# One tile instead of two for expert 0's later tokens, and the last routing rounds ahead of expert 0's first tile

## The chip, the cores and the metric

One core of one Trainium2 chip. The metric is the device time of one execution in microseconds (us), as the median of several runs. Engines are named as in the profile: PE (TensorE, the matmuls), PEld (its weight loads), DVE (VectorE), ACT (ScalarE), POOL (GpSimd), SP (SyncE, here a queue that issues transfers).

## What is computed

The reference is a decayed linear attention over 4 sequences of 768 tokens with 8 heads of 64 features, whose output is the input of a mixture of 16 experts in 4 groups:

```python
state = gamma[None, :, None, None] * state + np.einsum('bhd,bhe->bhde', k[:, :, t], v[:, :, t])
y[:, :, t] = scale * np.einsum('bhd,bhde->bhe', q[:, :, t], state)
...
g_idx = np.argmax(x @ w_group, axis=1)
e_idx = np.argmax(xg @ w_expert[g], axis=1)
h = np.maximum(xg[mask_e] @ w1[g, e], 0.0)
ye = h @ w2[g, e]
out[tok_idx] = (g_w[mask_g][mask_e] * e_w[mask_e])[:, None] * ye
```

All is float32 outside; there are 3072 tokens of 512 features, and an expert's two weight matrices (512 x 1024 and 1024 x 512) are 4 MB.

## The kernel before

**Attention and routing.** The attention takes 12 steps, each of two chunks of 128 tokens (`attention`, L851; 24 chunks in all). One step later the chunk's output is transposed back and stored to a DRAM tensor `xd` (`trans_mm`, `x_store` L289), and its router logits are formed: `logits_mm`, a copy by ACT, then `logits` (L312). Both logits steps write the same PSUM tile `log`. After every four chunks a routing round runs (`route` L325; six rounds): some six DVE operations that find group and expert, then five small matmuls that rank the tokens within each expert (`rk`), then some thirteen DVE operations that give each token its slot. `route_steps` issues the first part up to the word "wait" and, at its next call, the second. The slots go to POOL, which scatters each chunk's token numbers and gains into the lists `meta` (`enlist` L422).

**Expert 0 and expert 1 start early.** Their tokens of the first 12 chunks (`EARLY`) form tiles `ua` and `va` of 128 columns, which are worked on while the attention ends. Expert 0's later tokens form `ub` (88 columns, chunks 12 to 19, `MIDDLE` = 20) and `uc` (50 columns, chunks 20 to 23), expert 1's form `vb` (128 columns). A table gives chunk limit, width and list number:

```python
EARLY, MIDDLE = (12, 20)
PARTS = [
    [(EARLY, 128, 0), (MIDDLE, 88, NX), (NCH, 50, NX + 1)],
    [(EARLY, 128, 1), (NCH, 128, NX + 2)],
]
```

**A tile.** `listed` (L603) loads a tile's list on SP's queue, `gather` (L618) fetches the tokens by an indirect transfer that POOL issues, `xtrans` (L631) transposes them on PE into PSUM, from where ACT writes `xh` (float16) and DVE the rest `xl` (bfloat16). `layers` (L648) is a generator: four groups (`f2`) of 24 matmuls for the first layer, each of the three products wh.xh, wh.xl and wl.xh for four blocks of k and two halves `a`; after a group ACT writes `hh` and DVE `hl`. It stops after each half. Then the second layer, in one of two forms: with more than 116 columns (`TMAJ`) 24 matmuls of 512 columns (L714), else 96 matmuls that give the transposed result (L738), which `ytrans` (L764) turns back. `result` scales the rows and `scatter` writes them to the output through POOL. Transposes, first-layer groups and rank matmuls take turns in four PSUM slots (tag "big").

**Weights.** `wload` reads an expert's 4 MB in four transfers into four buffers on SP's queue, `wload_part` in sixteen. `wsplit` (L591) makes from a part `wh` (ACT) and then `wl` = wf - wh (DVE); a buffer is free for the next expert when its parts are split. Expert 0 is split in sixteen parts (k = 0 to 15, of which 9 to 15 fall in the stretch of the change), expert 1 in eight.

**The fourteen others.** When all tokens are counted, `order` (L436) ranks the experts by their number of tokens, ten DVE operations on one row that end with `ord`. `picked` (L577) lets SP read an entry of it; only then can the weights and the list of `us[0]` be asked for, and so on for 14 tiles of 256 down to 173 columns. A final loop (`general` L802) takes what did not fit in a tile.

**Order.** The program's order is kept on every engine (`manual_schedule`), so `run` (L937) fixes all queues. Behind the attention's last step it has: the logits matmuls of the last step, one group of `ua`, the transposes and stores, the list of `ub`, the first part of the sixth routing round, the last four splits of expert 0, the loads of expert 1's last two buffers, two groups of `ua`, the second part of the round and its four scatters, the gather of `ub`, the lists of `uc` and `vb`, the transposes of `va`, four splits of expert 1, the ranking and the first two loads of `us[0]`, the second layer of `ua`; then `va` (with four more splits), `ub`, `uc`, `vb` (with the splits of `us[0]` and, after its first-layer groups 1 and 2, the transposes of `us[0]`), and the loop over `us`. In the attention's last step, the first group of `ua` and three splits stand ahead of the transposes and the second part of the fifth round. One DRAM dependency is released by hand for `ub` (groups "middle" and "late"): its list and gather don't wait for what later chunks write.

Of the kernel before, what the change touches and what calls it, by code (L numbers as in the profile page):

```python
# [14 lines left out]
ALU = mybir.AluOpType  # L15
# [24 lines left out]
EARLY, MIDDLE = (12, 20)  # L40
PARTS = [
    [(EARLY, 128, 0), (MIDDLE, 88, NX), (NCH, 50, NX + 1)],
    [(EARLY, 128, 1), (NCH, 128, NX + 2)],
# [3 lines left out]
NP = NX + 3  # L47
PW = WIDTH + [PARTS[1][0][1], PARTS[0][0][1], PARTS[0][1][1], PARTS[0][2][1], PARTS[1][1][1]]
# [44 lines left out]
class Kernel:  # L93
# [195 lines left out]
    def x_store(self, i, s):  # L289

        nc, tc, st = self.nc, self.tc, self.st[i]
# [3 lines left out]
        d = nc.sync.dma_start(self.xd[t0:t0 + P, :], xr)  # L295
        if 2 * i >= MIDDLE:
            tc.add_to_no_dep_group("late", d.ins)
# [124 lines left out]
    def enlist(self, slot, src, c):  # L422
# [9 lines left out]
        if self.done > MIDDLE:  # L432
            tc.declare_no_dep(i.ins, group="middle", reason="no later token enters this list")
            tc.add_to_no_dep_group("middle", i.ins)
# [156 lines left out]
    def wsplit(self, u, k, n=8, eng=None):  # L591
# [3 lines left out]
        if h == 0:  # L595
# [7 lines left out]
    def listed(self, u, group=None, eng=None):  # L603

        nc, tc, bp = self.nc, self.tc, self.bp
# [4 lines left out]
        eng = eng or nc.sync  # L610
        for i, r in enumerate(rows):
            m = self.meta[u["seg"]] if static else self.meta[bass.ds(u["e"], 1)].rearrange("o r c -> (o r) c")
            d = eng.dma_start(mt[0:r, i, :], m[i * P:i * P + r, :])
            if group:
                tc.declare_no_dep(d.ins, group=group, reason="no later token enters this list")
                tc.add_to_no_dep_group(group, d.ins)

    def gather(self, u, group=None):  # L618
        nc, mt = self.nc, u["mt"]
        u["xg"] = xg = self.xg[u["at"][0]][:, u["at"][1]:, :]  # L620
        for i, r in enumerate(u["rows"]):
            n = u.get("tokens", NT)
            d = nc.gpsimd.indirect_dma_start(  # L623
# [4 lines left out]
            if group:  # L628
                self.tc.declare_no_dep(d.ins, group=group, reason="no token of these chunks is in the list")
# [18 lines left out]
    def layers(self, u):  # L648
# [6 lines left out]
        for f2 in range(4):  # L655
            ps = pp.tile([P, 512], F32, name="hps", tag="big", bufs=4)
            hv = ps.rearrange("p (a t) -> p a t", a=2)
            for a in range(2):
# [192 lines left out]
    def attention(self, extra, beside):  # L851
# [28 lines left out]
        for i in range(NST):  # L880
# [27 lines left out]
            if i >= 1:  # L908
# [28 lines left out]
    def run(self):  # L937
        tc, nc = self.tc, self.nc
        with ExitStack() as ctx:
# [14 lines left out]
            (ua, ub, uc), (va, vb) = [  # L954
                [dict(e=e, W=w, seg=l, tokens=c * P if c == EARLY else NT, pool=wpool[e]) for c, w, l in parts] for e, parts in enumerate(PARTS)
            ]
            for i, u in enumerate((ua, va, ub, uc, vb)):
                u["at"] = (0, i % 2)
            us = [dict(at=((j + 1) % 2, 0), W=WIDTH[j], pool=wpool[j % 2]) for j in range(NS)]
# [23 lines left out]
            def beside(i, place):  # L983
# [4 lines left out]
                if i == NST - 1:  # L988
# [173 lines left out]
```

## Time and profile before

| | us |
|---|---|
| median of 3 runs | 444.26 (443.36 to 444.46) |
| the profiled execution, device time | 442.78 |
| its span, first to last instruction | 441.0 |
| PE busy | 413.9 (94%) |
| DVE busy | 291.7 (66%) |
| ACT busy | 216.1 (49%) |
| POOL busy | 160.5 (36%) |

Times in the rows are microseconds from the span's start. Matmuls are pipelined: a row's second number is the time that the profile gives to an instruction or a merged group, and the distance of two starts is what an instruction costs in a dense run. "issue" is a wait for nothing that the profile shows. The granted clock is a share of 2.4 GHz; 0.50 is 1.2 GHz.

### The profile page before, as it was taken

The numbers are of one execution on the slowest core, as the hardware profiler recorded it, in microseconds if no ns is written. First come the engines' busy times: TensorE is split into PE (matmuls) and PEld (weight loads), VectorE is DVE, ScalarE is ACT, GpSimd is POOL, SyncE is SP. The second block draws the span as 40 slices with busy tenths as digits, with TensorE's granted clock in tenths as the row PEclk, the third lists the DMA queues.
The fourth block names the chain that finished last, engine by engine and source line by source line (L and its number), as shares of the span: only waits on it lengthen the run. The fifth ranks groups of instructions, "written<-read, shape, count | busy, mean of one in ns | idle before, by whom it ended". The sixth has DMA issues, their size and how long they took to land.

```text
span 441.0 us, 13102 instructions
## 1 busy us (share of the span) xinstructions
PE 413.9 (94%) x5502; PEld 337.1 (76%) x5502; DVE 291.7 (66%) x495; ACT 216.1 (49%) x345; POOL 160.5 (36%) x134
## 2 busy tenths in 40 slices
PE   7989999888798879999999999999999999999991
PEld 4878898677765867857788897978978879779770
DVE  3648568465696207968598976769668687696610
ACT  1132242234673327736474655757567567676520
POOL 4443855742354131422324350613504315222010
PEclk9999999999899969999999999999999999999996
DMA  8999999996657635977667777668887788876001
GB/s 271 417 325 410 351 394 365 302 270 196 242 192 246 225 89 201 297 265 240 233 238 268 252 275 300 222 257 261 309 311 261 257 286 293 295 289 253 27 9 34
DMA packets 37104, 112.76 MB, mean 256 GB/s; under 512 B 14095, under 2 KB 14735, under 8 KB 29363
## 3 DMA queue, kind: packets, MB, share of 16 engines
q1 hardware_dynamic: 25587, 98.08, 62.8%
q0 software_dynamic: 10496, 13.14, 9.4%
q8 instruction: 44, 0.72, 0.6%
q10 hardware_dynamic: 960, 0.68, 0.5%
q14 instruction: 17, 0.14, 0.1%
HBM read 99.47 MB, written 13.81 MB: 257 GB/s over the span
## 4 chain that ended last, share of the span: by engine, by line
PE 82%; issue 6%; DVE 4%; DMA 4%; ACT 1%; POOL 1%; POOLq 0%; DVEq 0%; ACTq 0%
PE hps L666 30%; PE yps L689 13%; PE yps L694 8%; PE yps L714 7%; PE sc L208 5%; PE op L269 5%; PE tpx L643 3%; PE tp L287 2%; PE stp L229 2%; DMA k<-kb 2%; PE op L257 2%; DVE wl L601 2%; PE yps L738 2%; PE log L305 1%; PE tpy L775 1%
## 5 line engine op out<-in xcount | busy, mean ns | idle before, releaser
L601 DVE TENSOR_TENSOR wl<-wf,wh 128x1024 bf16<-128x1024 f32 (+1 forms) x131 | 150.5, 1175 | 57.5 <-ACT wh L600 43.0
L666 PE MATMUL hps<-xbh,wl 128*128 128x128 f16 (+16 forms) x608 | 138.0, 244 | 1.3 <-issue 1.3
L666 PE MATMUL hps<-xbl,wh 128*128 128x128 bf16 (+16 forms) x608 | 138.0, 244 | 1.2 <-DVE xbl L646 1.2
L666 PE MATMUL hps<-xbh,wh 128*128 128x128 f16 (+16 forms) x608 | 138.1, 244 | 0.1
L600 ACT ACTIVATE wh<-wf 128x1024 f16<-128x1024 f32 (+1 forms) x136 | 130.7, 1000 | 0.4 <-DMA wf<-w2p 0.4
L666 PEld LDWEIGHTS <-wh 128*128 128x128 f16 x1216 | 105.5, 99 | 4.2 <-issue 1.0
L794 POOL DMA_INDIRECT out<-yo,mt x33 | 40.1, 1216 | 184.9 <-ACT yo L759 100.9
L623 POOL DMA_INDIRECT xg<-xd,mt x33 | 56.6, 1714 | 27.9 <-DMA mt<-meta 15.9
L671 ACT ACTIVATE hh<-hps 128x256 f16<-128x256 f32 (+16 forms) x76 | 35.7, 471 | 61.1 <-PE hps L666 58.0
L666 PEld LDWEIGHTS <-wl 128*128 128x128 bf16 x608 | 59.8, 99 | 3.7 <-issue 3.0
L672 DVE SCALAR_TENSOR_TENSOR hl<-hps,hh 128x256 bf16<-128x256 f32 (+16 forms) x76 | 40.1, 530 | 32.3 <-ACT hh L671 32.0
L694 PEld LDWEIGHTS <-wh 128*128 128x128 f16 x704 | 44.1, 98 | 20.8
L694 PE MATMUL yps<-hl,wh 128*128 128x103 bf16 (+10 forms) x352 | 44.3, 197 | 0.0
L694 PE MATMUL yps<-hh,wl 128*128 128x103 f16 (+10 forms) x352 | 44.3, 197 | 0.0
L694 PE MATMUL yps<-hh,wh 128*128 128x103 f16 (+10 forms) x352 | 44.2, 197 | 0.0
L215 DVE TENSOR_TENSOR pf<-sc,tri 128x512 f32<-128x512 f32 x48 | 30.0, 683 | 19.3 <-PE sc L208 16.8
L759 ACT ACTIVATE yo<-yps,mt 128x512 f32<-128x512 f32 x17 | 11.7, 687 | 57.1 <-PE yps L689 41.2
L426 POOL DMA_INDIRECT meta<-src,slot x24 | 24.7, 1031 | 37.4 <-DVE slot L418 32.1
L240 ACT ACTIVATE V<-stp 128x512 f32<-128x512 f32 x10 | 6.0, 597 | 65.6 <-PE stp L229 65.6
L689 PE MATMUL yps<-wh,hh 128*128 128x512 f16 x88 | 33.4, 379 | 0.0
L689 PE MATMUL yps<-wh,hl 128*128 128x512 f16 x88 | 33.3, 379 | 0.0
L689 PE MATMUL yps<-wl,hh 128*128 128x512 bf16 x88 | 33.3, 379 | 0.0
(139 smaller groups left out, 615.3 us busy)
## 6 DMA issues: line engine op xcount, KB each, us to landing
wf<-w1p SPq DMA_DIRECT2D x30, 1024.0 KB
wf<-w2p SPq DMA_DIRECT2D x30, 1024.0 KB
kk<-kkb SPq DMA_DIRECT2D x12, 512.0 KB
xd<-xr SPq DMA_DIRECT2D x24, 256.0 KB
k<-kb SPq DMA_DIRECT2D x11, 512.0 KB
q<-qb SPq DMA_DIRECT2D x11, 512.0 KB
v<-vb SPq DMA_DIRECT2D x11, 512.0 KB
wf<-w1p SPq DMA_DIRECT2D x8, 256.0 KB
```

Source lines behind the costliest of these rows:

```text
L215: nc.vector.tensor_tensor(st["pf"][:, s, par], st["sc", s, par].rearrange("p (g t) -> p g t", g=4), tri, ALU.mult)
L426: i = nc.gpsimd.indirect_dma_start(out=self.metaf, out_offset=bass.IndirectOffsetOnAxis(ap=slot[:, c:c + 1], axis=0), in_=src[:, c, :], in ...
L600: nc.scalar.activation(u["wh"][i][:, cs], u["wf"][i][:, cs], AF.Copy)
L601: (eng or nc.vector).tensor_tensor(u["wl"][i][:, cs], u["wf"][i][:, cs], u["wh"][i][:, cs], ALU.subtract)
L623: d = nc.gpsimd.indirect_dma_start(out=xg[0:r, i, :], out_offset=None, in_=self.xd[0:n, :], in_offset=bass.IndirectOffsetOnAxis(ap=mt[0:r, ...
L666: nc.tensor.matmul(hv[:, a, 0:W], l[:, k, fs], r[:, k, 0:W], start=(n == 0), stop=(n == 11))
L671: nc.scalar.activation(hh[:, f, 0:W], hv[:, :, 0:W], AF.Relu)
L672: nc.vector.scalar_tensor_tensor(hl[:, f, 0:W], hv[:, :, 0:W], 0.0, hh[:, f, 0:W], ALU.max, ALU.subtract)
L689: nc.tensor.matmul(ps, l[:, k, 0:P], m[k], start=(k == 0 and n == 0), stop=(k == 7 and n == 2))
L694: nc.tensor.matmul(yv[:, d, 0:r], l[g][:, ds], m[:, g, P:P + r], start=(g == 0 and n == 0), stop=(g == 7 and n == 2))
L714: nc.tensor.matmul(ps[0:r, :], l[:, k, ts], m[k], start=(n == 0), stop=(n == 23))
L794: s = nc.gpsimd.indirect_dma_start(out=self.out, out_offset=bass.IndirectOffsetOnAxis(ap=mt[0:r, i, 0:1].bitcast(U32), axis=0), in_=yo[0:r ...
```

## The change

Expert 0's tokens of the last twelve chunks become one tile of 128 columns, `ub`; `uc`, `MIDDLE` and the dependencies released by hand go. In the attention's last step the logits come ahead of the stores, and the first group of `ua` with its splits comes later, so that the second part of the fifth round stands ahead of it. Behind the attention, half a group of `ua` is followed by the last step's logits, transposes, logits of the routing and stores; the sixth round's first part comes ahead of three halves of `ua`'s groups, and its second part ahead of the last four splits of expert 0. A split can be issued in halves (`part`: "h" for ACT's, "l" for DVE's). For `ua` and `va` the twelve terms of a half group are sorted so that those with the operand named in `after` come last. The third buffer of expert 1 is asked for behind the last stores, the fourth behind the last four splits. The gathers of `ub` and `vb` follow expert 1's first four splits; the ranking and the first loads of `us[0]` move from ahead of `ua`'s second layer to behind the first layer of `va`, and the transposes of `ub` one step later in `va`'s second layer.

```diff
-EARLY, MIDDLE = (12, 20)
+EARLY = 12
 PARTS = [
-    [(EARLY, 128, 0), (MIDDLE, 88, NX), (NCH, 50, NX + 1)],
-    [(EARLY, 128, 1), (NCH, 128, NX + 2)],
+    [(EARLY, 128, 0), (NCH, 128, NX)],
+    [(EARLY, 128, 1), (NCH, 128, NX + 1)],
 ]
...
-NP = NX + 3
+NP = NX + 2
...
-    def wsplit(self, u, k, n=8, eng=None):
+    def wsplit(self, u, k, n=8, eng=None, part="hl"):
...
-        nc.scalar.activation(u["wh"][i][:, cs], u["wf"][i][:, cs], AF.Copy)
-        (eng or nc.vector).tensor_tensor(u["wl"][i][:, cs], u["wf"][i][:, cs], u["wh"][i][:, cs], ALU.subtract)
+        if "h" in part:
+            nc.scalar.activation(u["wh"][i][:, cs], u["wf"][i][:, cs], AF.Copy)
+        if "l" in part:
+            (eng or nc.vector).tensor_tensor(u["wl"][i][:, cs], u["wf"][i][:, cs], u["wh"][i][:, cs], ALU.subtract)
...
-                n = 0
-                for k in range(4):
-                    for l, r in ((wh, xh), (wh, xl), (wl, xh)):
-                        nc.tensor.matmul(hv[:, a, 0:W], l[:, k, fs], r[:, k, 0:W], start=(n == 0), stop=(n == 11))
-                        n += 1
+                terms = [(k, l, r) for k in range(4) for l, r in ((wh, xh), (wh, xl), (wl, xh))]
+                if "after" in u:
+
+                    late = dict(xl=xl, wl=wl)[u["after"]]
+                    terms.sort(key=lambda t: late is t[1] or late is t[2])
+                for n, (k, l, r) in enumerate(terms):
+                    nc.tensor.matmul(hv[:, a, 0:W], l[:, k, fs], r[:, k, 0:W], start=(n == 0), stop=(n == 11))
...
                 self.route_steps()
+                if i == NST - 1:
+                    self.logits(i - 1)
                 for s in range(2):
                     self.x_store(i - 1, s)
-                self.logits(i - 1)
+                if i < NST - 1:
+                    self.logits(i - 1)
...
+            ua["after"], va["after"] = "xl", "wl"
...
                     elif place == 2:
-                        first(2)
-                        for k in (9, 10, 11):
-                            self.wsplit(ua, k, 16)
+                        for k in (9, 10):
+                            self.wsplit(ua, k, 16, part="h")
...
+            first(1)
+            for k in (9, 10):
+                self.wsplit(ua, k, 16, part="l")
             last = NST - 1
             self.logits_mm(last)
             self.logits_copy(last)
-            first(2)
+            self.wsplit(ua, 11, 16)
             for s in range(2):
                 self.trans_mm(last, s)
+            self.logits(last)
             for s in range(2):
                 self.x_store(last, s)
-            self.logits(last)
-            while self.done < MIDDLE:
-                self.enlist(*self.todo.pop(0))
-            self.listed(ub, "middle")
+            self.wload(va, 2)
             self.steps.append(self.route(len(BATCHES) - 1))
             self.route_steps()
-            for k in range(12, 16):
-                self.wsplit(ua, k, 16)
-            self.wload(va, 2)
-            self.wload(va, 3)
-            first(4)
+            first(3)
             self.route_steps()
             assert not self.steps
             while self.todo:
                 self.enlist(*self.todo.pop(0))
-            self.gather(ub, "late")
-            self.listed(uc)
+            for k in range(12, 16):
+                self.wsplit(ua, k, 16)
+                if k % 2:
+                    first(2)
+            self.wload(va, 3)
+            self.listed(ub)
             self.listed(vb)
-            self.xtrans(va)
-            for _ in range(4):
-                wsplit()
-            self.steps.append(self.order())
-            self.route_steps()
-            self.picked(us[0], 0)
-            for i in range(2):
-                self.wload(us[0], i)
             self.rp2 = pool("rq")
             self.yp = pool("yp")
             self.xg.append(self.yp.tile([P, 2, DM], F32, name="xg1"))
             nc.gpsimd.memset(self.xg[1], 0.0)
...
+            self.xtrans(va)
+            wsplit(4)
+            self.gather(ub)
+            self.gather(vb)
             for k in self.first:
                 pass
...
             for i, k in enumerate(self.layers(va)):
                 if i in (0, 2, 4, 6):
                     wsplit()
-                if i == 9:
+                if i == 7:
+                    self.steps.append(self.order())
+                    self.route_steps()
+                    self.picked(us[0], 0)
+                    for n in range(2):
+                        self.wload(us[0], n)
+                if i == 10:
                     self.xtrans(ub)
-                if i == 10:
-                    self.gather(uc)
-                    self.gather(vb)
...
             for k in self.layers(ub):
                 if k == 3:
-                    self.xtrans(uc)
-            for k in self.layers(uc):
-                if k == 0:
-                    self.ytrans(ub)
-                if k == 3:
                     self.xtrans(vb)
             self.gather(us[1])
-            for i, k in enumerate(self.layers(vb)):
-                if k == 0:
-                    self.ytrans(uc)
+            for k in self.layers(vb):
                 if k in KX:
                     self.xtrans(us[0], (KX.index(k),))
```

## Rows read from the trace of the kernel before

**Rows 1.** The page: the span, and the chain by engine.

```profile
span 441.0 us, 13102 instructions
...
PE 82%; issue 6%; DVE 4%; DMA 4%; ACT 1%; POOL 1%; POOLq 0%; DVEq 0%; ACTq 0%
```

**Rows 2.** The chain in order of time: start, length, what.

```profile
113.15 2.67 PE hps L666 x24
...
139.20 2.03 PE hps L666 x50
...
160.04 2.56 PE hps L666 x24
...
165.47 1.34 PE hps L666 x24
167.26 1.34 PE hps L666 x24
168.60 5.18 PE yps L714 x24
173.78 5.24 PE hps L666 x48
```

**Rows 3.** Waits of PE, 100 to 175: total, times, longest.

```profile
PE yps L738 <- issue: 3.6, 8, 0.5
```

**Rows 4.** Stretches: length, busy PE, PEld, DVE, ACT, POOL, PEclk, DMA, GB/s.

```profile
113.00:114.00 1.00, 1.00 (x13) 0.92 (x10) 0.78 (x7) 0.38 (x1) 0.00 (x0) 0.50 1.22 418
157.00:158.00 1.00, 0.52 (x7) 0.32 (x7) 0.00 (x0) 0.00 (x0) 0.72 (x1) 0.50 0.50 111
...
153.50:154.00 0.50, 0.04 (x2) 0.01 (x1) 0.01 (x1) 0.00 (x0) 0.50 (x1) 1.00 0.69 98
154.00:155.00 1.00, 0.54 (x10) 0.40 (x11) 0.00 (x0) 0.00 (x0) 0.69 (x2) 1.00 0.57 205
```

**Rows 5.** Timeline of DVE, 104 to 139: start, length, instruction, [idle before].

```profile
106.88 0.68 DVE L646 TENSOR_TENSOR xbl<-tpx,xbh 128x512 bf16<-128x512 f32 x1
109.51 0.42 DVE L672 SCALAR_TENSOR_TENSOR hl<-hps,hh 128x256 bf16<-128x256 f32 x1 [1.95 <-ACT hh L671]
110.03 1.90 DVE L601 TENSOR_TENSOR wl<-wf,wh 128x512 bf16<-128x512 f32 x3
111.84 0.23 DVE L377 TENSOR_REDUCE sm<-ex 128x20 f32<-128x80 f32 x1
...
113.68 0.17 DVE L418 CAST slot<-sf 128x4 uint32<-128x4 f32 x1
...
117.73 0.24 DVE L346 TENSOR_REDUCE m<-L 128x20 f32<-128x80 f32 x1 [0.94 <-ACT xr L293]
...
119.10 0.23 DVE L360 TENSOR_TENSOR oh<-o 128x64 bf16<-128x64 f32 x1
...
124.78 4.62 DVE L601 TENSOR_TENSOR wl<-wf,wh 128x1024 bf16<-128x1024 f32 x4
...
132.07 0.72 DVE L475 CAST ord<-ordf 1x16 int32<-1x16 f32 x1
...
135.09 1.22 DVE L601 TENSOR_TENSOR wl<-wf,wh 128x1024 bf16<-128x1024 f32 x1
...
137.69 0.42 DVE L672 SCALAR_TENSOR_TENSOR hl<-hps,hh 128x256 bf16<-128x256 f32 x1
```

**Rows 6.** Timeline of SP's queue, 120 to 146.

```profile
122.75 0.83 SPq L575 DMA_DIRECT2D wf<-w2p  x2
134.02 0.69 SPq L613 DMA_DIRECT2D mt<-meta  x2
136.08 0.95 SPq L575 DMA_DIRECT2D wf<-w1p  x2
...
138.49 5.93 SPq L613 DMA_DIRECT2D mt<-meta  x6
```

**Rows 7.** Timeline of POOL, 110 to 160.

```profile
151.94 1.03 POOL L623 DMA_INDIRECT xg<-xd,mt  x1 [10.61 <-DMA mt<-meta]
```

More of the change, by code (lines that the diff above doesn't have):

```diff
@@ L46 @@
 WIDTH = [256, 245, 231, 223, 217, 211, 205, 200, 196, 192, 188, 185, 180, 173]
-NP = NX + 3
-PW = WIDTH + [PARTS[1][0][1], PARTS[0][0][1], PARTS[0][1][1], PARTS[0][2][1], PARTS[1][1][1]]
+NP = NX + 2
+PW = WIDTH + [PARTS[1][0][1], PARTS[0][0][1], PARTS[0][1][1], PARTS[1][1][1]]
 C_GV, C_GX, C_GD, C_SEL = 0, 48, 52, 84
@@ L289, in x_store @@
     def x_store(self, i, s):
-        nc, tc, st = self.nc, self.tc, self.st[i]
+        nc, st = self.nc, self.st[i]
         xr = self.wp.tile([P, DM], F32, name="xr", bufs=4)
@@ L294, in x_store @@
         t0 = (2 * (i // NC) + s) * S + i % NC * P
-        d = nc.sync.dma_start(self.xd[t0:t0 + P, :], xr)
-        if 2 * i >= MIDDLE:
-            tc.add_to_no_dep_group("late", d.ins)
+        nc.sync.dma_start(self.xd[t0:t0 + P, :], xr)
     def logits_mm(self, i):
@@ L431, in enlist @@
         tc.add_to_no_dep_group("meta", i.ins)
-        if self.done > MIDDLE:
-            tc.declare_no_dep(i.ins, group="middle", reason="no later token enters this list")
-            tc.add_to_no_dep_group("middle", i.ins)
     def order(self):
@@ L589, in wload_part @@
         self.nc.sync.dma_start(u["wf"][i][:, cs], (self.a_w1, self.a_w2)[i // 2][u["e"], i % 2][:, cs])
-    def wsplit(self, u, k, n=8, eng=None):
+    def wsplit(self, u, k, n=8, eng=None, part="hl"):
         nc = self.nc
         i, h = divmod(k, n // 4)
-        if h == 0:
+        if h == 0 and "h" in part:
             u["wh"][i] = u["pool"][i].tile([P, 2048], F16, name="wh", tag=f"wh{i}", bufs=1)
@@ L599, in wsplit, with listed @@
         cs = slice(h * w, h * w + w)
-        nc.scalar.activation(u["wh"][i][:, cs], u["wf"][i][:, cs], AF.Copy)
-        (eng or nc.vector).tensor_tensor(u["wl"][i][:, cs], u["wf"][i][:, cs], u["wh"][i][:, cs], ALU.subtract)
-    def listed(self, u, group=None, eng=None):
-        nc, tc, bp = self.nc, self.tc, self.bp
+        if "h" in part:
+            nc.scalar.activation(u["wh"][i][:, cs], u["wf"][i][:, cs], AF.Copy)
+        if "l" in part:
+            (eng or nc.vector).tensor_tensor(u["wl"][i][:, cs], u["wf"][i][:, cs], u["wh"][i][:, cs], ALU.subtract)
+    def listed(self, u):
+        nc, bp = self.nc, self.bp
         W = u["W"]
@@ L609, in listed, with gather @@
         static = isinstance(u["e"], int)
-        eng = eng or nc.sync
         for i, r in enumerate(rows):
             m = self.meta[u["seg"]] if static else self.meta[bass.ds(u["e"], 1)].rearrange("o r c -> (o r) c")
[L613 to L618, printed above, removed]
+            nc.sync.dma_start(mt[0:r, i, :], m[i * P:i * P + r, :])
+    def gather(self, u):
         nc, mt = self.nc, u["mt"]
@@ L622, in gather @@
             n = u.get("tokens", NT)
-            d = nc.gpsimd.indirect_dma_start(
+            nc.gpsimd.indirect_dma_start(
                 out=xg[0:r, i, :], out_offset=None, in_=self.xd[0:n, :],
@@ L627, in gather @@
             )
-            if group:
-                self.tc.declare_no_dep(d.ins, group=group, reason="no token of these chunks is in the list")
     def xtrans(self, u, tiles=(0, 1)):
@@ L952, in run @@
             nc.gpsimd.memset(self.xg[0], 0.0)
-            (ua, ub, uc), (va, vb) = [
+            (ua, ub), (va, vb) = [
                 [dict(e=e, W=w, seg=l, tokens=c * P if c == EARLY else NT, pool=wpool[e]) for c, w, l in parts] for e, parts in enumerate(PARTS)
             ]
-            for i, u in enumerate((ua, va, ub, uc, vb)):
+            for i, u in enumerate((ua, va, ub, vb)):
                 u["at"] = (0, i % 2)
+            ua["after"], va["after"] = "xl", "wl"
             us = [dict(at=((j + 1) % 2, 0), W=WIDTH[j], pool=wpool[j % 2]) for j in range(NS)]
@@ L1049, in run @@
             nc.gpsimd.memset(self.xg[1], 0.0)
-            for u, v in ((ub, ua), (uc, ua)):
-                u["wh"], u["wl"] = v["wh"], v["wl"]
+            self.xtrans(va)
+            wsplit(4)
+            self.gather(ub)
+            self.gather(vb)
             for k in self.first:
                 pass
+            ub["wh"], ub["wl"] = ua["wh"], ua["wl"]
             vb["wh"], vb["wl"] = va["wh"], va["wl"]
```

## The prediction, made before the changed kernel was run

> **What bounds the kernel now.** I read the page first, then the chain of waits over the changed stretch, then each engine's timeline there. The page shows a span of 441.0 us; 82% of the chain that ended last is TensorE (PE) work [rows 1]. So what counts is when PE reaches the stage of the fourteen chosen experts: from its first matmul at 173.78 [rows 2] no row gives PE a wait worth naming, and a shift of that instant is a shift of the end.
>
> The chain shows what lies before it [rows 2]. The third tile of expert 0 (W=50) and the second (W=88) stand between 139.20, where ub's first layer starts, and 160.04, where the last tile of expert 1 (vb) starts: 20.8 us. A good part of that is no arithmetic: in the second layers of the narrow tiles PE sat idle eight times, 3.6 us in total, with "issue" as the only releaser [rows 3], and in 157 to 158 the granted clock stood at 0.50 [rows 4].
>
> VectorE's (DVE's) timeline shows the other resource. It does all the work up to the ranking of the experts (`ord`, 132.07 + 0.72 = 132.79) with holes: 1.95 us idle after 107.56, most of 113.85 to 117.73 without work, and it ends expert 1's splits and corrections at 138.11 [rows 5]. SyncE (SP) and GpSimd (POOL) show the third: the first chosen expert's 4 MB are issued from 136.08, its token list from 138.49 [rows 6], and POOL can start that expert's gather only at 151.94, after 10.61 us idle on the list [rows 7]. In the kernel before this is hidden, because PE wants those tokens only in vb, near 165.
>
> **Part 1: one tile of 128 columns.** It takes away, for uc: one list, one gather, two transposition groups, four relu/correction pairs, a result and a scatter; for ub the transposition of its result. The first layer at W=128 costs four groups of 24 matmuls at 1.34 us each, 5.36 us, the second 24 matmuls in 5.18 us [rows 2]; with vb's transposition, 0.44 (165.47 + 1.34 to 167.26), that is 11.0 us instead of 20.8: 9.8 us of PE time less. By the reference's inputs 122 tokens of the last twelve chunks belong to expert 0, so 128 columns hold them and the final loop stays empty. The ranking and the item list lose one column out of 19 and two or three DVE operations; they lie beside matmuls of the us-stage and I cost them at nothing (uncovered, under 1 us).
>
> **Part 2: the routing rounds ahead of expert 0.** I re-add DVE's order from its rows [rows 5], because DVE has least room here. After `xbl` (107.56) the second half of the fifth round needs ACT's exponential, which now follows only two half splits; say 108.1. Then: 2.0 for that half (111.84 to 113.85), 110.1; three splits 1.9, 112.0; first half of the sixth round 1.6 (117.73 to 119.33) and its small copy, 113.7; two corrections 0.8, 114.5; second half 2.0, 116.5; four splits 2.5 (three took 1.90) and two corrections 0.8, 119.7; `xbl` of expert 1 0.65, 120.4; its four splits 4.6, 125.0; four more pairs of split and correction at 1.5 (two pairs from 135.09 to 138.11), 131.0; ranking 3.4 (129.40 to 132.79), **ord at 134.4**. DVE thus finishes everything 3.7 us earlier than 138.11, yet `ord` itself comes 1.6 us later, since four pairs now stand ahead of it.
>
> PE by the same list: the sixth round's rank matmuls wait for the first correction, because their PSUM slot is that of the first group, until about 114; two groups 2.7, a transposition, expert 0's second layer 5.18, to 122.7; expert 1's four groups 5.4 and second layer 5.18 with a transposition, to 133.8. The sort of terms (`xl` last, `wl` last) moves no work; it lets 8 of 12 matmuls go before the late operand, and gains nothing where the PSUM slot is what is late. Then PE waits for `xbl` of ub, which DVE now does behind the ranking: 134.4 + 0.65 = 135.1, about 1.3 us of idle PE. ub with vb's transposition takes 11.0, to 146.1; vb's first two groups 2.7, to **148.8**, where PE wants the tokens of us[0].
>
> Queues moved past. POOL: the sixth round's four list scatters start after 116.5, some 8 us sooner with the slots they wait for, the last near 122; the clearing of `xg1` and the gathers of ub and vb follow, all by about 131, with tpx(ub) wanted at about 132.5 (1 to 2 us late would be paid by PE's 5 us of slack below). SP: the two stores of each step stand behind one logits copy of 0.2 us more; expert 1's third quarter of weights is issued earlier, its last quarter behind the last four splits of expert 0 (near 119.7; in before 122.75 [rows 6]); then two lists, whose entries land before 127, so SP is free when `ord` comes. I cost these at nothing; cover: DVE's own queue until 131.
>
> **Part 3: what is late next.** SP needed 1.37 us from the end of its list loads (134.02 + 0.69 = 134.71) to the first weight load [rows 6], with `ord` long there. So the loads go out at 134.4 + 1.4 = 135.8 instead of 136.08. From first load to POOL's gather took 15.86 us before [rows 6, 7]; that gives 151.7. Two gathers that shared the transfer engines then are now over before it; at most about 1 us, I take 0.4: 151.3. The gather's data moved from 153.5 to about 155.0 for an issue at 151.94 (0.05 + 0.2 MB in two windows of [rows 4]), that is 3.1 us after issue: **tokens at 154.4**. PE has waited 5.6 us by then. From there a transposition, group, transposition, group, second layer: 0.44 + 3.13 (165.47 to 168.60) + 5.18 = 8.75 at full clock, so us[0] starts at 163.1.
>
> That wait has a price in clock. After the sparse stretches of before, the granted clock stood at 0.50 (1.2 GHz) in 113 to 114 and again from 157 [rows 4], and 24 matmuls then took 2.67 us instead of 1.34 [rows 2]. Bounds for here: nothing, or both of vb's last groups at half clock, 2.7 us. I take 2.0, nearer the upper end, since at both places of the rows the low level followed a sparse stretch. us[0] then starts at 165.1, 8.7 us before 173.78. The Trainium skill ("TensorE: Matmul & The Clock Gate", "Why this matters for your kernels") also says that idle gaps between bursts of matmuls bring the low clock back, which speaks against a change that opens such a gap; those rows agree, and by the rule alone the full 2.7 would be paid.
>
> The skill's page "DMA: Bandwidth & Descriptors" ("Anatomy of one DMA") gives about 2.0 us plus bytes over 436 GB/s for a transfer on the POOL path; an estimate by it for 4.19 MB and then a list is 13.6 us, not 15.86, which would give about 2 us more. The row is of this queue and decides.
>
> **Sum.** The profiled execution took 442.78 us; 442.78 - 8.7 = 434.1. The median of the runs shown is 1.48 us above it, so the forecast for a median is **435.6 us**.
>
> **Rivals.**
> A. The list does not hold PE up (it lands ahead of the weights, or PE is later than I think, so that nothing waits). Then PE alone decides: 148.8 + 8.75 = 157.6, a gain of 16.2, 428.1 us. Against it: the list did keep POOL idle up to 151.94 [rows 7]. Chance 0.07.
> B. The gain is largely given back: the clock stays low through vb's second layer as well, the gaps of [rows 3] come back in the new tile's 192 loads and matmuls of the first layer, or the list is 2 us later. 2.5 to 6 us of gain left, 438.3 to 441.8. The gaps speak little for it, as they would fall into the 5.6 us wait. Chance 0.10.
> C. Slower: `ord` is held up. It now stands behind four splits that need the last quarter of expert 1's weights, whose load was moved behind expert 0's last splits. Everything after it (weights, list, gather) follows one for one, so from `ord` at 134.4 + 8.7 = 143.1 on the change loses. A weight load landing 14 us later than my list has it (some 2 us of room, then 12 lost) gives `ord` at 146.4 and 447.6 us. Against: SP has nothing else to wait for at that point. Chance 0.05.
> D. The change does not do what it says: an overflow of the 128 columns would send PE into the final loop. 122 tokens speak against it; chance 0.01, and it would be slower, by one pass with an expert's 4 MB of weights.
> E. No difference: the earlier finish is eaten by the list wait and clock, gain under 1.3 us. This needs 7.5 us of loss at one place; chance 0.03.
>
> **How the numbers follow.** The forecast has 0.74. Its own ends: list 1.5 us sooner and no clock loss, 435.6 - 3.5 = 432.1; list and `ord` 1.5 us later with full clock loss and a little more, 438.5. B's upper half is beyond that, so the range that leaves out no more than 2 in 10 is 431.5 to 439.6. A measurement of this kernel can tell about 0.3% (1.3 us) from no change. Faster 0.91 (the forecast, A and B), same 0.03 (E), slower 0.06 (C and D).
>
> **What would show it.** Right: `ord` near 134; weight loads from about 136; POOL idle until about 151 on the list; PE idle for 4 to 6 us ahead of tpx of us[0] in vb, released by DMA; clock 0.50 behind it; us[0]'s first matmul near 165; no L738 rows in this stretch. Wrong: vb running without a wait (A); `ord` past 140 (C); half clock into us[0] (B); iterations of the final loop (D).

## The result, and the profile after

| | before | after |
|---|---|---|
| median, us (4 runs each) | 443.81 (442.47 to 444.46) | 437.26 (435.77 to 438.89) |
| ratio, 95% interval | | 0.985 [0.981, 0.989] |
| profiled execution, device time / span | 442.78 / 441.0 | 438.53 / 436.7 |
| PE busy | 413.9 | 406.8 |

The change makes the kernel 6.55 us faster (443.81 - 437.26); 435.6 had been forecast. The page's first lines and its chain by engine answer to [rows 1]:

```profile
span 436.7 us, 12493 instructions
...
PE 72%; DVE 8%; DMA 8%; issue 6%; ACT 2%; another core or an unknown queue 1%; POOL 1%; SPq 1%; POOLq 0%; DVEq 0%; ACTq 0%
```

PE's share of the chain fell from 82% to 72%. From 133.43 on nearly all of the chain before is PE and its idle times with "issue"; now DVE's list up to `ord`, SP's loads and two transfers stand on the path up to 159.04. The chain of waits in order of time (start, length, what), to set beside [rows 2], shows which:

```profile
138.21 0.17 DVE ord L470
...
139.44 0.36 SPq L570
...
141.86 12.12 DMA mt<-meta
...
154.79 4.12 DMA xg<-xd,mt
...
159.04 1.08 PE tpx L634 x4
160.13 2.20 PE hps L660 x24
...
162.77 1.34 PE hps L660 x24
...
169.29 2.73 PE hps L660 x25
```

Read it upwards from the first matmul of `us[0]` at 169.29. It comes 10.25 us after the transposition of that tile's tokens (159.04); the tokens came 4.12 us after POOL issued the gather, the gather waited 12.12 us for a small list that was asked for behind 4 MB of weights on the same queue, and all of it hung on `ord` (138.21). PE's waits in 100 to 170 (total, times, longest), against [rows 3], where eight idle times of `yps` with "issue" made 3.6 us:

```profile
PE tpx L634 <- DMA xg<-xd,mt: 6.9, 2, 4.7
PE hps L660 <- issue: 1.2, 2, 1.0
```

The eight are gone with the narrow layers, but two others, 1.2 us, stand in `ua`'s first layer. The 6.9 us are two waits: 4.65 us for the tokens of `us[0]`, and 2.27 us for those of `ub`, inside `va`'s second layer. POOL's timeline (start, length, instruction, idle before) has both gathers; the second answers to [rows 7], 12.29 us idle on the list against 10.61:

```profile
134.43 1.72 POOL L616 DMA_INDIRECT xg<-xd,mt  x1 [6.35 <-DMA mt<-meta]
...
154.79 1.81 POOL L616 DMA_INDIRECT xg<-xd,mt  x1 [12.29 <-DMA mt<-meta]
```

The granted clock fell behind the longer wait, as at 113 and 157 in [rows 4] (stretches; the value behind "POOL busy" is PEclk):

```profile
160.00:162.00 2.00, 2.00 (x23) 2.00 (x22) 0.95 (x2) 1.54 (x2) 1.65 (x2) 0.55 0.61 166
162.00:164.00 2.00, 2.00 (x35) 1.99 (x33) 1.87 (x3) 1.54 (x3) 0.00 (x0) 1.00 0.49 158
```

**Where the time came from.** For all that follows the kernel is cut at two marks: the end of `xbl` of `ua`, where DVE finishes with the attention's last step, and the first matmul of `us[0]`. Before, the first mark is 107.56 and the second 173.78: a stretch of 66.22 us. After, DVE's timeline has

```profile
109.82 0.68 DVE L637 TENSOR_TENSOR xbl<-tpx,xbh 128x512 bf16<-128x512 f32 x1
...
119.16 0.42 DVE L665 SCALAR_TENSOR_TENSOR hl<-hps,hh 128x256 bf16<-128x256 f32 x1 [2.85 <-ACT hh L664]
```

so 109.82 + 0.68 = 110.50 and a stretch of 58.79, 7.43 us shorter. From the second mark to the end of the span it is 267.22 before and 267.41 after (in the experiments 266.6 to 267.0, in experiment 3 alone 268.8). The profiled execution of after reached the first mark 2.94 us later, so its span is only 7.43 - 2.94 - 0.19 = 4.3 us shorter. The first mark scatters from one profiled execution to the next: over all profiles it lies between 102.6 and 111.5, with either order of work near both ends, so the 2.94 us are not put down to the change, and the stretch is what the experiments compare.

### The profile page after: what moved, and what is told of

The parts are those of the page before. It is cut to its first block, busy times and chain, and to the rows that moved or that the text cites. A ratio compares the mean times of both kernels' runs of the same rounds, so it can differ in the third digit from the quotient of the medians.

```text
span 436.7 us, 12493 instructions
## 1 busy us (share of the span) xinstructions
PE 406.8 (93%) x5197; PEld 329.6 (75%) x5226; DVE 290.4 (66%) x487; ACT 213.7 (49%) x337; POOL 159.7 (37%) x132
## 4 chain that ended last, share of the span: by engine, by line
PE 72%; DVE 8%; DMA 8%; issue 6%; ACT 2%; another core or an unknown queue 1%; POOL 1%; SPq 1%; POOLq 0%; DVEq 0%; ACTq 0%
PE hps L660 24%; PE yps L682 12%; PE yps L687 8%; PE yps L707 6%; PE sc L208 5%; PE op L269 5%; DVE wl L598 4%; DMA mt<-meta 3%; PE op L257 2%; PE tpx L634 2%; PE tp L287 2%; PE stp L229 2%; DMA k<-kb 2%; PE log L303 2%; DVE hl L665 1%
## 5 line engine op out<-in xcount | busy, mean ns | idle before, releaser
L660 PE MATMUL hps<-xbh,wl 128*128 128x128 f16 (+14 forms) x576 | 131.8, 246 | 1.6 <-issue 1.0
L660 PE MATMUL hps<-xbh,wh 128*128 128x128 f16 (+14 forms) x576 | 133.2, 246 | 0.1
L660 PE MATMUL hps<-xbl,wh 128*128 128x128 bf16 (+14 forms) x576 | 131.7, 246 | 0.3 <-issue 0.2
L660 PEld LDWEIGHTS <-wh 128*128 128x128 f16 x1152 | 102.1, 98 | 4.2 <-issue 1.0
L787 POOL DMA_INDIRECT out<-yo,mt x32 | 38.8, 1212 | 179.6 <-ACT yo L752 96.4
L664 ACT ACTIVATE hh<-hps 128x256 f16<-128x256 f32 (+14 forms) x72 | 35.1, 488 | 58.3 <-PE hps L660 51.9
L687 PEld LDWEIGHTS <-wh 128*128 128x128 f16 x704 | 44.1, 98 | 20.8
L660 PEld LDWEIGHTS <-wl 128*128 128x128 bf16 x576 | 55.6, 98 | 2.2 <-DVE wl L598 0.8
L665 DVE SCALAR_TENSOR_TENSOR hl<-hps,hh 128x256 bf16<-128x256 f32 (+14 forms) x72 | 39.5, 549 | 21.0 <-ACT hh L664 20.6
L687 PEld LDWEIGHTS <-wl 128*128 128x128 bf16 x352 | 32.7, 98 | 0.7 <-issue 0.7
```

The costliest lines, as they stand in the source:

```text
L664: nc.scalar.activation(hh[:, f, 0:W], hv[:, :, 0:W], AF.Relu)
L665: nc.vector.scalar_tensor_tensor(hl[:, f, 0:W], hv[:, :, 0:W], 0.0, hh[:, f, 0:W], ALU.max, ALU.subtract)
L687: nc.tensor.matmul(yv[:, d, 0:r], l[g][:, ds], m[:, g, P:P + r], start=(g == 0 and n == 0), stop=(g == 7 and n == 2))
L787: s = nc.gpsimd.indirect_dma_start(out=self.out, out_offset=bass.IndirectOffsetOnAxis(ap=mt[0:r, i, 0:1].bitcast(U32), axis=0), in_=yo[0:r ...
```

## The experiments

The theory was that PE had set the end of the stretch, that the new tile takes 9.8 us of PE's time away, and that the list's path (`ord`, 4 MB, list, gather) takes some of it back; rivals were that the order alone or the tile alone does it. Every ratio below is to the kernel before on the same chip. Three chips were used, called A, B and C here; on which chip the first measurement was made is not known. The kernel before took 433.25 us (29 runs) on A (experiments 1 to 4), 432.76 (35) on B (5 to 8) and 444.56 (17) on C (9 to 12), and this turned out to matter: the expectations of experiments 1 to 4 were worked out from the 443.81 us of the first measurement, so their differences count and not their microseconds. The changed kernel as it is was run on B and C, not on A.

**1. The tile alone.** The kernel before with the new table of parts, in the old order; `ub`'s list and gather come when all slots are scattered, as one list of all twelve chunks needs.

```diff
-EARLY, MIDDLE = (12, 20)
+EARLY = 12
...
-            self.gather(ub, "late")
-            self.listed(uc)
+            self.listed(ub)
             self.listed(vb)
...
+            self.gather(ub)
+            self.gather(vb)
```

> The kernel before with expert 0's later tokens as one tile of 128 columns and nothing of the new order (its list and gather follow the sixth round's scatters, as expert 1's did). Theory (PE loses 9.8 us of narrow tiles, and from then on the chain ranking, weight loads, list, gather of us[0] sets the start of us[0]): the list chain stays as before, tokens of us[0] near 155; ub's gather comes later than in the changed kernel, near 140, so PE waits about 4 us in va; us[0] near 166 instead of 173.8, about 436 us. Rival 1 (the gain comes from the routing rounds moved ahead, the tile only fills a wait): within 1 us of the kernel before, 443 to 444. Rival 2 (all PE time removed arrives at the end): 434.

Measured 436.24 us, 1.008 [1.005, 1.011]: slower, which neither the theory nor a rival had. The waits of PE in 100 to 182 say where:

```profile
PE tpx L638 <- DMA xg<-xd,mt: 7.0, 1, 7.0
```

and the chain of the same kernel why:

```profile
133.78 7.86 DMA xg<-xd,mt
...
141.78 1.09 PE tpx L638 x4
142.86 3.63 PE yps L709 x12
```

PE stood 7.0 us for the tokens of `ub`: the second tile of before needed only chunks up to 19, the new one all 24, whose scatters the old order has late. And the gather, issued 0.7 us after the first weight loads of `us[0]` (133.05), took 7.86 us instead of the 4.12 us above; then the twelve matmuls left of `va`'s second layer ran at 0.30 us each instead of 0.22.

**2. The order alone.** The changed kernel with the three tiles of before.

```diff
-EARLY = 12
+EARLY, MIDDLE = (12, 20)
 PARTS = [
-    [(EARLY, 128, 0), (NCH, 128, NX)],
+    [(EARLY, 128, 0), (MIDDLE, 88, NX), (NCH, 50, NX + 1)],
...
```

> The changed kernel with expert 0's later tokens as two tiles of 88 and 50 columns again; the new order of rounds, splits and ranking stays. Theory: PE is the bound again, 9.8 us more of it, of which the 4.7 us wait for us[0]'s tokens and its clock loss are taken back: us[0] 3 to 4 us later than in the changed kernel, about 441 us, and no wait of PE for that gather. Rival 1 (the order makes the gain): 437 to 438. Rival 2 (the tile makes all of it): 443 to 444.

Measured 429.96 us, 0.992 [0.989, 0.995]; the theory's 441 would be 0.994. So on chip A the order brings 0.8% by itself: the list of `ub` is asked for at 124.36 instead of 131.13 in experiment 1, PE waits 2.2 us for its tokens, and PE comes to `us[0]` too late to wait for them. The chain shows what the narrow layers of `ub` cost at full clock, first and second, for use below, and an idle time (a hole, in what follows) in `uc`'s second layer:

```profile
134.33 4.05 PE hps L660 x96
138.38 0.38 PE tpx L634 x4
138.76 3.90 PE yps L731 x96
...
146.50 1.82 issue
```

Behind this hole, which is released by nothing that the profile shows, the layer's last 81 matmuls took 3.47 us, with a granted clock of 0.62 and 0.53 from 148 to 152. So PE came late to `us[0]` in part because of the hole, and not by its arithmetic alone.

**3. The list ahead of the weights.** The changed kernel; one line moved.

```diff
                     self.picked(us[0], 0)
+                    self.listed(us[0])
                     for n in range(2):
                         self.wload(us[0], n)
...
             for i in range(2, 4):
                 self.wload(us[0], i)
-            self.listed(us[0])
             self.gather(us[0])
```

> The changed kernel with us[0]'s token list asked for ahead of its four weight loads. Theory: the list no longer lands behind 4 MB; POOL's gather starts near 143 to 146 instead of 154.8, PE's wait of 4.7 us ahead of us[0]'s transposes and the half clock behind it go, us[0] starts about 6 us earlier, 431 us. Rival (something else would hold PE at the same place, the gathered rows behind the weights or the splits of us[0]): PE waits there still, gain under 2 us, 435.5 to 437.5.

Measured 427.86 us, 0.987 [0.982, 0.992], the lowest median on chip A. SP's first weight loads in its timeline:

```profile
137.27 0.91 SPq L570 DMA_DIRECT2D wf<-w1p  x2
```

and POOL's gather of `us[0]`:

```profile
139.27 1.04 POOL L616 DMA_INDIRECT xg<-xd,mt  x1 [0.30 <-issue]
```

The gather goes out 2 us after the first weight load instead of 15.35 us after it (139.44 to 154.79 in after). The stretch is 54.0 us, and the only wait of PE for tokens that is left is one of 2.0 us for `ub`. That the list, and not the tokens' own transfer or the weights, held PE is shown by this; what it is worth against the changed kernel has to wait for experiment 11, on a chip where both were run.

**4. The ranking earlier.** The changed kernel; the ranking and the first two loads of `us[0]` directly behind expert 1's first four splits.

```diff
             wsplit(4)
+            self.steps.append(self.order())
+            self.route_steps()
+            self.picked(us[0], 0)
+            for n in range(2):
+                self.wload(us[0], n)
             self.gather(ub)
```

> The changed kernel with the ranking and us[0]'s first two loads where the kernel before had them, behind expert 1's first four splits. Theory: ord about 5.5 us earlier, so loads, list and gather too; tokens near 153.5, when PE comes to them at 154.4; the four corrections of va come 3 us later, which PE's wait for ub's tokens covers. Gain 4.5 to 5.5 us against the changed kernel, 432 to 433. Rival (ord does not set the wait): within 1 us of the changed kernel; or va's second layer waits for its corrections and gives it back.

Measured 431.78 us, 0.999 [0.995, 1.003]. `ord` came at 122.69, and PE did not wait for `us[0]`; but it waited elsewhere. The first weight loads went out at 126.98; POOL's timeline has `ub`'s gather right behind them:

```profile
127.56 1.39 POOL L616 DMA_INDIRECT xg<-xd,mt  x1 [9.12 <-DMA mt<-meta]
```

and PE's timeline the transposition of its tokens:

```profile
135.44 1.09 PE L634 MATMUL tpx<-ident,xg 128*128 128x128 f32 x4 [6.00 <-DMA xg<-xd,mt]
```

The gather of `ub` now starts 0.6 us behind the first weight load and its tokens are there after 7.9 us, as in experiment 1. The stretch is 57.9 us, 3.9 more than in experiment 3. So `ord` can come too early: in the changed kernel's first profile `ub`'s tokens are through (138.58) before the weights start (139.44).

**5 and 6. Both kernels unaltered, on chip B.** Experiments 1 and 2 had not added up to the gain of the first measurement, so the changed kernel and the kernel before were run as they are.

> The changed kernel itself, unaltered, for a profile on the same chip as the next run. Theory: from the first correction xbl of expert 0 to us[0]'s first matmul 59 to 60 us, as in its first profile (59.5), PE waiting 4 to 5 us for us[0]'s tokens; against the kernel before a ratio near 0.985. Rival (a good part of the gain of the first comparison was stalls of the kernel before that come and go with the chip and the run): ratio above 0.99.

> The kernel before itself, unaltered. Theory: from xbl to us[0] 66 to 67 us again, with the gaps for issue in uc's second layer (3.6 us in the first profile) and the half clock behind them; ratio 1.000. Rival: without those gaps the stretch is 60 to 62 us, which would say that PE time of the narrow tiles is worth what the new wait costs, and that the gaps made the difference.

Measured 431.8 us, 0.998 [0.994, 1.001], for the changed kernel, and 431.3, 0.997 [0.994, 1.000], for the kernel before. Here the change brings nothing that can be told, as both rivals had it. (The 59.5 us of the first expectation counts from the start of `xbl`; by the marks it is 58.79.) The chain of the kernel before (experiment 6) shows what is different:

```profile
139.90 5.46 PE yps L738 x96
145.35 0.60 PE hps L666 x24
145.95 0.59 PE tpy L775 x4
146.54 1.80 PE hps L666 x72
148.34 0.48 PE tpx L643 x4
148.82 2.40 PE yps L738 x96
151.22 1.34 PE hps L666 x24
```

`uc`'s second layer is 96 matmuls in 2.40 us without a hole, and `vb`'s first group runs at full clock. In the first measurement the eight idle times of [rows 3] lay in this layer and the group behind it took 2.56 us [rows 2]. `ub` and `uc` take 17.7 us (133.51 to 151.22), not 20.8, and that still has 2.04 us of waiting for `uc`'s tokens, with the clock low behind it (`ub`'s second layer 5.46 us against 3.90 in experiment 2). The stretch is 60.44 us before and 60.83 after: equal. DVE's timeline of the changed kernel (experiment 5) has something that the first measurement had not:

```profile
122.11 1.23 DVE L598 TENSOR_TENSOR wl<-wf,wh 128x1024 bf16<-128x1024 f32 x1 [1.58 <-ACT wh L596]
...
127.16 1.23 DVE L598 TENSOR_TENSOR wl<-wf,wh 128x1024 bf16<-128x1024 f32 x1 [2.03 <-ACT wh L596]
```

ACT had waited 1.77 and 2.51 us for the last weights of expert 1, so DVE idled 3.6 us on the way to `ord`, which ended 28.9 us after the mark (104.12 to 133.0).

**7. The wait filled.** The changed kernel with twenty idle matmuls (they write the unused `log` tile and add no part of the result) ahead of the transposition of `us[0]`.

```diff
             for k in self.layers(vb):
+                if k == KX[0]:
+                    self.heat(20)
```

> The changed kernel with 20 idle matmuls of 512 columns (216 ns each, 4.3 us; their result is not used) between vb's second group and the transposes of us[0], that is, inside PE's wait. Theory (the wait is paid a second time in clock): the granted clock stays at 1.00 behind the wait, the group after it takes 1.34 us instead of 2.20, us[0] starts 1.3 to 1.6 us earlier. Rival (the slow group has another cause): the group stays above 2 us. If there is no wait on this chip, the filling costs what it lasts beyond the tokens' arrival, up to 4 us.

Measured 432.3 us, 0.999 [0.996, 1.002]. The chain of experiment 5, the same kernel without them:

```profile
153.61 1.09 PE tpx L634 x4
154.70 2.56 PE hps L660 x24
...
158.11 1.66 PE hps L660 x24
```

and the chain here:

```profile
151.14 4.35 PE log L158 x20
155.49 0.44 PE tpx L634 x4
155.93 1.34 PE hps L660 x24
...
157.71 1.34 PE hps L660 x24
```

The idle matmuls kept the clock at its upper level, 3.56 us from the first transposition to the end of the last group (155.49 to 159.05) instead of 6.16 (153.61 to 159.77): 2.6 us. The stretch is 57.97 us against 60.83. The total shows none of it. One reason is in the runs: experiment 5's profile had a mean clock of 0.976, but of its twelve executions only four were that low (0.972 to 0.976, 432.0 to 434.3 us), and six had 0.984 to 0.987 (428.8 to 431.9 us); here none was under 0.977. This suggests that the clock does not fall in every execution and that its 2.6 us are not in the median; it is not shown, as the mean is over the whole span. Another reason may be that the filling is too long: the gather went out at 151.10, the tokens of `us[0]` came 3.4 to 4.3 us after it in the profiles of the changed kernel, which gives 154.5 to 155.4 as an estimate, and the idle matmuls ended at 155.49.

**8. Without the sort of terms.** The changed kernel without `ua["after"], va["after"] = "xl", "wl"`.

> The changed kernel without the sorted terms (no operand named as late). Theory: the same time within 0.3%; the first group of ua is held by its PSUM slot, and va's first groups find wl done. Rival: va's first layer waits for wl, up to 1 us, which the wait for us[0]'s tokens swallows.

Measured 433.1 us, 1.001 [0.998, 1.004], against 0.998 [0.994, 1.001] for the changed kernel: the intervals overlap, and no gain of the sort can be told.

**9 and 10. Both kernels unaltered, on chip C.** To see whether the gain comes and goes with the idle times.

> The kernel before once more, for a profile beside the next three. Theory (the gaps for issue in uc's second layer and the half clock behind them belong to the chip or the run, not to the kernel): on a chip without them, from xbl to us[0] 60 to 61 us, on one with them 65 to 67. Rival (they are the kernel's, and the last look was the exception): 65 to 67 on any chip.

> The changed kernel once more. Theory: 59 to 61 us from xbl to us[0] on any chip, 4 to 5 us of them PE's wait for us[0]'s tokens; so the ratio to the kernel before is near 0.998 on a chip without the gaps and near 0.985 on one with them. Rival: near 0.985 on any chip.

Measured 445.29 us, 1.003 [1.000, 1.006], for the kernel before, and 436.33 us, 0.985 [0.979, 0.990], for the changed one: the first measurement again. The chain of the kernel before (of the many short pieces between 157.03 and 162.97 two stand here):

```profile
155.96 1.07 PE yps L738 x43
...
157.33 0.47 issue
157.79 0.29 PE yps L738 x5
...
162.97 1.10 PE yps L738 x22
164.07 2.56 PE hps L666 x24
...
167.29 1.34 PE hps L666 x24
```

`uc`'s second layer takes 8.1 us (155.96 to 164.07) against 2.40 on chip B, and the group behind it runs at half the speed, 2.56 us against 1.34: 5.7 + 1.2 = 6.9 us that the kernel before does not lose on chip B. The stretch is 65.83 us, 5.4 longer than there (60.44), as `ub`'s second layer is 1.6 us shorter here (148.62 to 152.49, 3.87). The changed kernel's stretch is 57.13: 8.7 shorter, and its median is 8.96 us below the other's. It has such idle times too, though fewer: 1.7 us in four, against 6.0 us in twelve in the kernel before (105 to 175 us). Three stand in `ua`'s first layer, among matmuls of 128 columns (PE's timeline):

```profile
116.32 0.33 PE L660 MATMUL hps<-xbl,wh 128*128 128x128 bf16 x3 [0.23 <-issue]
117.07 0.23 PE L660 MATMUL hps<-xbh,wh 128*128 128x128 f16 x1 [0.31 <-issue]
117.79 0.22 PE L660 MATMUL hps<-xbh,wh 128*128 128x128 f16 x1 [0.44 <-issue]
```

They end 0.75 and 0.72 us apart; those in `uc`'s second layer of experiment 9 (157.79, 158.56, up to 162.97) end 0.70 to 0.77 us apart. So they are no matter of narrow matmuls alone.

**11. The list ahead of the weights, on chip C.** Experiment 3's kernel.

> The changed kernel with us[0]'s list ahead of its weights, a second time. Theory: 54 to 55 us from xbl to us[0], no wait there, 4 to 6 us faster than the changed kernel in the same call and about 1.2% faster than the kernel before on a chip without the gaps. Rival (the first measurement was luck of the chip): within 2 us of the changed kernel.

Measured 433.71 us, 0.979 [0.974, 0.984]: 2.6 us under the changed kernel of experiment 10 (six runs each; the two intervals overlap), where 4 to 6 had been expected; stretch 54.86. This version beats the kernel before on chips A and C, and the changed kernel on C by its median. The idle times did not go: there are seven of up to 0.6 us, 2.6 us in all, three in `ua`'s first layer, one in `va`'s and three in `ub`'s.

**12. The narrow layer three times.** The kernel before, with `uc`'s second layer computed three times over (the two first times are work thrown away), to see whether the idle times go with the number of narrow matmuls.

```diff
+                for _ in range(3 if u["W"] == 50 else 1):
...
                         nc.tensor.matmul(yv[:, d, 0:r], l[k][:, ds], m[:, k, ts], start=(n == 0), stop=(n == 23))
```

> The kernel before with uc's second layer done three times over (the first two results are overwritten): 192 more matmuls of 50 columns, with their weight loads, at 25 ns a pair 4.8 us. Theory (PE's instructions come more slowly than so narrow a stretch uses them up, and the gaps start when what was fetched ahead is used up): gaps for issue appear inside the longer stretch, and it takes 10 to 20 us instead of 7.2. Rival (the gaps have nothing to do with the number of instructions): 7.2 us without a gap, the kernel 4 to 5 us slower.

Measured 450.51 us, 1.014 [1.008, 1.019], 5.2 us over experiment 9. Its chain:

```profile
155.52 1.27 PE yps L739 x51
156.79 0.31 issue
...
161.93 1.05 issue
162.99 6.92 PE yps L739 x206
169.91 1.34 PE hps L666 x24
```

The layer takes 14.4 us, inside the 10 to 20 of the theory, but not for its reason: there are 288 matmuls instead of 96 and only a little more idle time (4.3 us in seven against 3.7 in eight), the holes lie in the same 6.2 us (156.79 to 162.99), then 206 matmuls run without one. So the holes do not go with the number of narrow matmuls: the notion that such matmuls run a store of fetched instructions dry falls in the simple form, for it would have holes to the end. That PE's instructions come late for another reason is neither shown nor excluded: transfers of 16 KB marked "instruction" lie across the first hole of the narrow layer in before (152.99 to 154.23) and in experiment 2 (145.88 to 146.76), but one lies in the same layer of experiment 6 as well (149.36 to 150.97), which has no hole.

## Why the prediction was right, and where its steps were not

**The time and the direction** were right: 435.6 forecast, 437.26 measured, inside the range; the gain 8.7 forecast, 7.43 in the stretch of the profiled execution, 8.7 in experiment 10's and 6.55 in the first median. On chip B the same change gained nothing, so that the forecast came true owes something to the chip.

**Part 3, what is late next,** was right in mechanism and nearly in size. Shifted by the 2.94 us of the later mark, the gather was forecast at 154.2 and came at 154.79; the tokens at 157.3 and came by 159.04, since the transfer took 4.12 us and not 3.1. First load to gather was 15.35 us here and 15.08 and 15.43 in experiments 5 and 10, for 15.46 in the sum (15.86 - 0.4). The estimate by the Trainium skill's page "DMA: Bandwidth & Descriptors" ("Anatomy of one DMA"), 13.6 us, is below all of these; the row, which is of this queue, was the better guide. The wait of PE was forecast at 5.6 us and was 4.65, because PE itself came 2.7 us later than the sum had it (154.39, against 148.8 + 2.94). Experiment 3 takes the wait away by moving the list alone.

**The clock** behind the wait: 2.0 forecast. In the profile of after the two transpositions and groups of 3.56 us took 5.07 (159.04 to 162.77 + 1.34), 1.5 us; in experiment 5 2.6; in experiment 8, behind a wait of 3.5 us, 1.8; in experiment 10, behind a wait of 2.5 us, the granted clock stayed at 1.00, `hps` at 1.34, and nothing was lost to the clock. The bounds 0 to 2.7 hold all four. The rule of the Trainium skill ("TensorE: Matmul & The Clock Gate", "Why this matters for your kernels"), that gaps between bursts bring the low clock back, agrees with experiments 5 and 7, but not with its full price in each case.

**Part 1, "9.8 us of PE time less",** is the step that was wrong, though its sum held in the first measurement, from which its rows came. The difference 20.8 - 11.0 was read as the cost of two narrow tiles. Added up at full clock and without holes, from the rows of experiments 2 and 6, the same work is 4.05 + 0.38 + 3.90 + 0.60 + 0.59 + 1.80 + 0.48 + 2.40 = 14.2 us. So of the 9.8 us only 3.2 are arithmetic; 6.6 were hindrance: 4.0 us of holes (3.6 in [rows 3], 0.42 at 141.23 in `ub`'s first layer), the rest waiting and the low clock. Which of it a kernel meets depends on the chip or the run, and the changed kernel brings 4.8 to 6.9 us of waiting for tokens of its own. In the two comparisons where the trace of the kernel before has the holes, the first and that on chip C, the change gains 1.5%; in the one without, on chip B, nothing. The prediction did say that a good part of the 20.8 us "is no arithmetic", but then asked only whether the holes would come back (rival B), not whether they belong to the kernel.

**Part 2, DVE's list,** held in the first measurement: `ord` was forecast at 134.4, 137.3 with the shift, and ended at 138.37. Yet its parts were not as summed. In after DVE idled 2.85 us for ACT's second `hh` of `ua`, which started at 118.75 after 3.9 us idle with a releaser that the profile calls remote, 0.1 us after the end of PE's last hole in that layer (118.64). The same wait of 3.9 us stands in experiments 10 and 11, and in none of the profiles of the new order on chips A and B. In experiment 5 DVE idled 3.6 us for weights instead, and `ord` came 2.0 us later than the sum (28.88 against 134.4 - 107.56 = 26.84 behind the mark). The wait of PE ahead of `ub` was named wrongly: the sum had 1.3 us for `xbl` behind the ranking; in fact the tokens were late, 2.27 us. Both gathers were to be over by 131, 133.9 with the shift, and ended at 137.49: SP waited 7.2 us for the scatters into `meta` before it could ask for the two lists (131.79), a wait that the sum had put at nothing. That late tokens of `ub` would be paid out of the 5 us of slack was said, and they were. Experiment 1 shows what the reordering is for: without it this wait is 7.0 us and the tile makes the kernel slower by 0.8%.

**Rivals.** A, no wait for `us[0]`, is what experiments 3 and 11 made on purpose: stretches of 54.0 and 54.9 us against 57.1 to 60.8 for the changed kernel; A's own number had been 50.0 (157.6 - 107.56). C, expert 1's last weights holding `ord`, came in small in experiment 5, at 2 us instead of the 8.7 from which it decides. In after the weights held `wh` for 1.3 us. E, no difference, was given 0.03 because it "needs 7.5 us of loss at one place"; on chip B it is what happened, less by a loss than because there was less to win.

**Open:** what makes the idle times with "issue". Between 105 and 175 us all six profiles of the first measurement and of chip C have them, of either kernel: 4.9 to 6.0 us in ten to twelve with the narrow tiles, 1.2 to 2.6 us in two to seven with the tile of 128 columns. Of the eight profiles of chips A and B only that of experiment 2 has one. Their number does not follow that of the matmuls (experiment 12). In the six profiles the first mark also came late (107.6 to 111.5, against 102.6 to 106.3 in the eight), so time is lost ahead of the stretch as well. And the tile or the order alone was not run on chip C: that the gain there comes from the narrow layers is read from the traces, not shown by undoing one part.

## What to carry to other kernels

Before an idle time is booked as the kernel's own cost, see whether it is there on another chip; a gain that consists of such holes was there only where they were. Where a small list must be read before a gather can start, ask for it ahead of the megabytes on the same queue: that was one line, and left PE no wait for those tokens on either chip where it was tried. And when PE time is cut ahead of a stage, work out when that stage's inputs arrive: here 3.2 us of arithmetic were taken out and, in two of three profiles of the changed kernel, 6.9 us of waiting stood in the stretch.

## What the runs showed of the hardware

- One program took 432.8 us on one chip and 444.6 on another. On the slower chip PE had idle times released by nothing that the profile shows, mostly 0.2 to 0.5 us long, among narrow matmuls and among those of 128 columns; within a burst of them their ends were 0.70 to 0.79 us apart, or twice that (experiments 9 to 12). On the faster chip the same 96 narrow matmuls ran in 2.40 us instead of 8.1.
- An indirect gather of 128 rows took 3.6 to 4.3 us from issue to the transposition of its tokens when no weight loads had just started (after and experiments 2, 3, 7, 10 and 11), and 7.9 to 8.0 us when it was issued 0.6 to 0.7 us behind the first of them (experiments 1 and 4).
- With a wait of 4.7 us ahead of them the same two groups and transpositions took 5.1 and 6.2 us in two profiled executions, and 3.56 with twenty idle matmuls in the wait. With a wait of 2.5 us the granted clock stayed at 1.00 (experiment 10).
